# A root of one-tensor steps, and a new order of all operations and buffers, in a fused attention and two-layer kernel

## The chip, the cores and the metric

The kernel runs on one core of a Trainium2 chip. The metric is the device time of one execution in microseconds. Three runs of the kernel before took 750.36, 754.2 and 755.68 us; their median, 754.2 us, is what the change is measured against.

## The reference, cut to what matters

Windowed attention (4 batches, 8 heads, 576 positions, head size 64, window 128, a slope per head), then a layer with a softmax-weighted activation and a layer norm, then a second layer with a sigmoid gate. There are 2304 tokens of 512 numbers; the weights are float64 in memory.

```python
scores = scale * (q @ k.T) + slope * -|rel|, masked to 0 <= rel < 128
attn_out = softmax(scores) @ v                       # 2304 x 512
h = attn_out @ w_in                                  # 512 -> 1024
solu = h * softmax(h)
ln = (solu - mean(solu)) / np.sqrt(var(solu) + 1e-06) * g_ln
x2 = ln @ w_out                                      # 1024 -> 512
h2 = x2 @ w2_in                                      # 512 -> 2048
out = (h2 * (1 / (1 + np.exp(-h2)))) @ w2_out        # 2048 -> 512
```

## The kernel before, in words

**Numbers.** Every matmul operand is split into two fp16 parts, high and low, and a product takes three matmuls (high by high, high by low, low by high). The weights arrive as 64-bit words: `decode` (L404 to L411) makes float32 of them on DVE in three instructions per tile of 128x512, 48 tiles in all (8 of w_in, 8 of w_out, 16 of w2_in, 16 of w2_out). A weight's scale needs the norm over all of its tiles (squares on ACT, summed on PE at L449), so no tile of a matrix is split before the whole matrix is decoded. `split_weight` (L457) splits a tile in one of two ways, by a letter of `E_W`: V is one ACT instruction (L469) and one DVE instruction (L471); G is two ACT instructions (L475, L335) and one on POOL (L340).

**Stages.** The tokens are 18 blocks of 128. A block goes through attention (four pairs of heads: scores L599, bias and maximum L624, exp L629, high and low part of the result L335 with L339 or L340, a transposing DMA L656, product with v L676), is divided by its sums (xm, L689), split and transposed (x, L704, or on PE at L504), multiplied by w_in (L718), and normalised (`layer_norm`, L722 to L776). Two blocks make a chunk, nine chunks in all. A chunk is multiplied by w_out (`m1_out`, L808, into the tile y), then goes in eight groups through w2_in (`m2_in`, L845, gate at L854 to L858, into the tile g) and w2_out (`m2_out`, L872).

**The root in the layer norm.** The inverse root of the variance is a guess by bit operations (L747, L749) and three Newton steps, each of two `scalar_tensor_tensor` instructions on 128x1 tiles (L751, L753). Both have two tensors as inputs; L751 has a pointer to a scalar besides, L753 an immediate. L757 is of the form of L751.

**Order.** Every operation is recorded with a priority and with the engines that may do it, and a list planner on the host (`Sched.solve`, L178) gives out the order: at each moment the engine that can begin first takes the ready operation with the lowest priority number. The priority is `PITCH * i + RANK[kind]` for a block i, or a number of `WAT` for weight tiles (the first for load and decode, the third for the split). DMAs are issued by SP, in the same order. `ENG` chooses, per block, whether the subtraction for the low part of a (attention), x or l (normalised rows) goes to V (DVE), G (POOL) or B (the planner chooses); `ON_PE` chooses per block whether x or l is transposed on PE (P) or by DMA (D). The `N_...` constants are the numbers of buffers of a tile: a buffer is written again only when all readers of its last contents are done. For a group of `m2_in` that is a buffer of PSUM ("mm", 2), one of t (`N_T`), one of g (`N_G`); for a chunk one of lnT and one of y.

## Time and profile before

| | |
|---|---|
| median of three runs | 754.2 us |
| the profiled execution | 753.94 us, span 752.2 us, mean granted clock 0.972 |
| PE busy | 679.7 us (90%) |
| DVE busy | 467.9 us (62%) |
| ACT busy | 392.6 us (52%) |
| POOL busy | 68.4 us (9%) |
| chain that ended last | PE 73%, DVE 15%, DMA 5%, ACT 3% |

The span is what the profile covers, from the first instruction to the last; the execution's own time has 1.7 us more. Busy shares are means over the whole span; in slices of a fortieth, PE stands at 2 to 6 tenths in the first slices and at 9 from the ninth on (with an 8 in the tenth and in the last), and DVE the other way round, at 8 or 9 in most of the first third and at 1 to 3 at the end.

### The profile page before, as it was taken

The numbers are of one execution on the slowest core, as the hardware profiler recorded it, in microseconds if no ns is written. First come the engines' busy times: TensorE is split into PE (matmuls) and PEld (weight loads), VectorE is DVE, ScalarE is ACT, GpSimd is POOL, SyncE is SP. The second block draws the span as 40 slices with busy tenths as digits, with TensorE's granted clock in tenths as the row PEclk, the third lists the DMA queues.
The fourth block names the chain that finished last, engine by engine and source line by source line (L and its number), as shares of the span: only waits on it lengthen the run. The fifth ranks groups of instructions, "written<-read, shape, count | busy, mean of one in ns | idle before, by whom it ended". The sixth has DMA issues, their size and how long they took to land.

```text
span 752.2 us, 13817 instructions
## 1 busy us (share of the span) xinstructions
PE 679.7 (90%) x5366; PEld 453.7 (60%) x5366; DVE 467.9 (62%) x1259; ACT 392.6 (52%) x843; POOL 68.4 (9%) x63
## 2 busy tenths in 40 slices
PE   2445568898999999999999999999999999999998
PEld 1121235676764776567675775686666768767763
DVE  5998989989999867645466546646553272322221
ACT  6588558777677765444363535634661251322231
POOL 0053013312213000000020000000110000000000
PEclk9998668999999999999999999999999999999999
DMA  8997896579753646055342350464232300300000
GB/s 233 283 261 210 248 241 129 131 195 199 186 99 84 155 98 148 1 93 121 69 99 58 85 99 15 99 120 78 57 85 51 62 30 1 57 29 1 1 29 29
DMA packets 144034, 80.28 MB, mean 107 GB/s; under 512 B 125920, under 2 KB 126560, under 8 KB 143968
## 3 DMA queue, kind: packets, MB, share of 16 engines
q1 hardware_dynamic: 143968, 79.39, 44.9%
q8 instruction: 42, 0.69, 0.4%
q14 instruction: 24, 0.20, 0.1%
HBM read 44.24 MB, written 4.72 MB: 65 GB/s over the span
## 4 chain that ended last, share of the span: by engine, by line
PE 73%; DVE 15%; DMA 5%; ACT 3%; issue 2%; SPq 1%; POOL 0%; DVEq 0%; ACTq 0%; POOLq 0%
PE mm L872 23%; PE mm L845 22%; PE mm L808 11%; PE mm L718 9%; PE sa L599 4%; PE sa L676 3%; DMA stage<-in_moe_w_in_dram 2%; DVE bits L407 2%; DVE bits L409 2%; DVE W L411 2%; DVE e L624 2%; DMA aT<-a 1%; DMA stage<-in_moe_w_out_dram 1%; DVE W L471 1%; DVE e L739 1%
## 5 line engine op out<-in xcount | busy, mean ns | idle before, releaser
L845 PE MATMUL mm<-y,W 128*128 128x256 f16 x1728 | 208.4, 273 | 3.4 <-DVE t L855 2.0
L872 PE MATMUL mm<-W,g 128*128 128x512 f16 x864 | 206.8, 379 | 0.0
L845 PEld LDWEIGHTS <-W 128*128 128x128 f16 x1728 | 166.2, 98 | 41.4 <-issue 3.8
L872 PEld LDWEIGHTS <-g 128*128 128x128 f16 x864 | 81.8, 98 | 78.7 <-issue 0.6
L718 PE MATMUL mm<-W,xT 128*128 128x512 f16 x432 | 107.3, 395 | 1.6 <-ACT xT L506 1.3
L808 PE MATMUL mm<-lnT,W 128*128 128x256 f16 x864 | 106.9, 276 | 0.0
L808 PEld LDWEIGHTS <-W 128*128 128x128 f16 x864 | 84.2, 99 | 18.7 <-issue 0.3
L629 ACT ACTIVATE e<-e,mx 128x256 f32<-128x256 f32 (+1 forms) x144 | 70.0, 487 | 34.7 <-DVE mx L624 34.4
L599 PEld LDWEIGHTS sa<-k,q 64*128 64x128 f32 x544 | 41.6, 209 | 62.9 <-DVE mx L624 34.2
L857 ACT ACTIVATE g<-t 128x512 f16<-128x512 f32 x72 | 44.9, 625 | 66.2 <-PE mm L872 54.1
L858 DVE SCALAR_TENSOR_TENSOR g<-t,g 128x512 f16<-128x512 f32 x72 | 49.5, 688 | 47.4 <-ACT g L857 47.0
L855 DVE SCALAR_TENSOR_TENSOR t<-t,mm 128x512 f32<-128x512 f32 x72 | 48.8, 683 | 47.0 <-ACT t L854 47.0
L599 PE MATMUL sa<-k,q 64*128 64x128 f32 x544 | 57.1, 329 | 19.2 <-DVE mx L624 13.1
L718 PEld LDWEIGHTS <-xT 128*128 128x128 f16 x432 | 42.1, 101 | 51.8 <-issue 8.0
L854 ACT ACTIVATE t<-mm,cs 128x512 f32<-128x512 f32 x72 | 48.5, 679 | 46.5 <-PE mm L845 46.4
L624 DVE CUSTOM_DVE_ANT_0 e<-sa,table 128x256 f32<-128x256 f32 (+1 forms) x144 | 55.7, 404 | 23.6 <-PE sa L599 9.7
L335 ACT ACTIVATE a<-e 128x512 f16<-128x512 f32 (+1 forms) x72 | 43.1, 598 | 36.2 <-DMA aT<-a 35.9
L340 POOL TENSOR_TENSOR a<-e,a 128x512 f16<-128x512 f32 x24 | 29.0, 1210 | 290.9 <-ACT a L335 256.6
L449 PE MATMUL mm<-sq,ones 128*128 128x512 bf16 x32 | 17.0, 537 | 39.2 <-ACT sq L439 32.1
L339 DVE TENSOR_TENSOR a<-e,a 128x512 f16<-128x512 f32 (+1 forms) x48 | 31.5, 656 | 26.3 <-ACT a L335 26.3
L816 DVE SCALAR_TENSOR_TENSOR y<-mm,cs,y 128x512 f16<-128x512 f32 x18 | 13.4, 748 | 48.9 <-ACT y L813 48.9
L813 ACT ACTIVATE y<-mm,cs 128x512 f16<-128x512 f32 x18 | 12.3, 686 | 57.2 <-PE mm L808 49.1
(124 smaller groups left out, 698.0 us busy)
## 6 DMA issues: line engine op xcount, KB each, us to landing
stage<-in_moe_w_in_dram SPq DMA_DIRECT2D x24, 512.0 KB, 5.1
stage<-in_moe_w_out_dram SPq DMA_DIRECT2D x24, 512.0 KB, 4.2
vraw<-in_vt_dram SPq DMA_DIRECT2D x34, 256.0 KB, 3.4
k<-in_kn_dram SPq DMA_DIRECT2D x18, 256.0 KB, 3.1
q<-in_qn_dram SPq DMA_DIRECT2D x18, 256.0 KB, 3.5
out_dram<-t SPq DMA_DIRECT2D x18, 256.0 KB, 2.0
aT<-a SPq DMA_TRANSPOSE x72, 3.1
lnT<-ln SPq DMA_TRANSPOSE x34, 3.2
```

Source lines behind the costliest of these rows:

```text
L335: "A": ("A", ca(n), lambda: A.activation(dst(), src(), AF.Copy), False)}
L599: T.matmul(SA[:, j, sl * P:(sl + 1) * P], q[rows, p, :], k[rows, p, :], start=True, stop=sl not in blank)
L624: v(n + 75, lambda j=j: V.tensor_tensor_reduce(e[:, j, lo:lo + n], SA[:, j, lo:lo + n], table[:, 2 * p + j, o:o + n], -0.125, 3.0e38, ALU. ...
L629: act(n, lambda j=j: A.activation(e[:, j, lo:lo + n], e[:, j, lo:lo + n], AF.Exp, bias=mx[:, j:j + 1], scale=-1.0, accum_out=rs[:, 2 * p + ...
L718: T.matmul(pt[:, half * 512:(half + 1) * 512], x[:, hx, k, :], W16(2 * k + half, hw), start=(k == 0 and hx + hw == 0), stop=(k == KD - 1 a ...
L808: T.matmul(pt[:, ct % 2], W16(8 + k, hw)[:, ct * P:(ct + 1) * P], l[:, hx * KF1 + k, :], start=(k == 0 and hw + hx == 0), stop=(k == KF1 - ...
L845: T.matmul(pt[:, mm], W16(16 + 4 * k + m // 4, hw)[:, (m % 4) * P:(m % 4 + 1) * P], y[:, hx, k, :], start=(k == 0 and hw + hx == 0), stop= ...
L854: act(512, lambda: A.activation(t.tile, flat(pt.tile), AF.Tanh, scale=cs[:, 0:1]), [pt, (cs, 0)], [t], extra=1)
L855: v(512, lambda: V.scalar_tensor_tensor(out=t.tile, in0=t.tile, scalar=1.0, in1=flat(pt.tile), op0=ALU.add, op1=ALU.mult), [t, pt], [t])
L857: act(512, lambda: A.activation(flat(g[:, 0]), t.tile, AF.Copy, scale=2.0 ** -16), [t], [(g, 0)])
L858: v(512, lambda: V.scalar_tensor_tensor(out=flat(g[:, 1]), in0=t.tile, scalar=2.0 ** -16, in1=flat(g[:, 0]), op0=ALU.mult, op1=ALU.subtrac ...
L872: T.matmul(pt.tile, g[:, hg, mm, b * P:(b + 1) * P], W16(32 + m, hw), start=(m == 0 and hg + hw == 0), stop=(m == KF2 - 1 and hg == 1))
```

## The change

The root's steps become `tensor_scalar` instructions: one tensor and two scalars, of which both are pointers in the first step (var and y) and one in the second (y). The sign that the reversed subtraction gave moves into the constant in front of the steps. The instruction that makes `share` (L757) takes the same form. The planner's costs of five kinds of instruction are changed, and all numbers that set the order: pitch, ranks, the weights' priorities, the choices of engine, the numbers of buffers and `AHEAD`. The table of biases gets a rank of its own. Nothing else of the computation changes.

```diff
@@ -481,6 +481,7 @@
 
 
     def make_table():
+        s.at("table", 0)
         r = Buf(early, [P, 512, 2], U32, "stage", N_STAGE)
 
         def rl():
@@ -561,7 +562,7 @@
         sv = rows_of(i, v_scale, "sv")
         r = vraw.pop(i)
         act(512, lambda: A.activation(t[:, :, 0, :], r.tile, AF.Identity, scale=sv.tile), [r, sv], [(t, 0)], extra=1)
-        v(570, lambda: V.scalar_tensor_tensor(out=t[:, :, 1, :], in0=r.tile, scalar=sv.tile, in1=t[:, :, 0, :],
+        v(640, lambda: V.scalar_tensor_tensor(out=t[:, :, 1, :], in0=r.tile, scalar=sv.tile, in1=t[:, :, 0, :],
                                               op0=ALU.mult, op1=ALU.subtract), [r, sv, (t, 0)], [(t, 1)], port=True)
 
 
@@ -621,7 +622,7 @@
         else:
             lo, n, o = cur, P, P
         for j in range(2):
-            v(n + 75, lambda j=j: V.tensor_tensor_reduce(
+            v(n + 20, lambda j=j: V.tensor_tensor_reduce(
                 e[:, j, lo:lo + n], SA[:, j, lo:lo + n], table[:, 2 * p + j, o:o + n], -0.125, 3.0e38,
                 ALU.add, ALU.min, mx[:, j:j + 1]), [(SA, ("s", j)), (table, 2 * p + j)], [(e, j), (mx, j)])
         s.at("exp", i, p)
@@ -729,7 +730,7 @@
         if i % 2 == 0:
             share[i // 2] = Buf(const, [P, 2], F32, "share", 2)
         sh = share[i // 2]
-        v(1024, lambda: V.tensor_reduce(mx(), pt.tile, AX.X, ALU.max), [pt], [st])
+        v(1090, lambda: V.tensor_reduce(mx(), pt.tile, AX.X, ALU.max), [pt], [st])
         v(60, lambda: V.tensor_scalar(mx(), mx(), sg[:, 1:2], None, ALU.mult), [st, sg], [st])
         act(1024, lambda: A.activation(e.tile, pt.tile, AF.Exp, bias=mx(), scale=sg[:, 0:1], accum_out=sm()),
             [pt, st, sg], [e, st], extra=2.6)
@@ -746,16 +747,14 @@
           [st], [st])
         v(1, lambda: V.tensor_scalar(y().bitcast(U32), var().bitcast(U32), 1, 0x7FFFFFFF,
                                      ALU.logical_shift_right, ALU.bitwise_xor), [st], [st])
-        v(1, lambda: V.tensor_scalar(y(), y(), 0.7 * 2.0 ** -65.5, None, ALU.mult), [st], [st])
+
+        v(1, lambda: V.tensor_scalar(y(), y(), -0.7 * 2.0 ** -65.5, None, ALU.mult), [st], [st])
         for _ in range(3):
-            v(110, lambda: V.scalar_tensor_tensor(out=w(), in0=y(), scalar=var(), in1=y(), op0=ALU.mult,
-                                                  op1=ALU.mult), [st], [st])
-            v(80, lambda: V.scalar_tensor_tensor(out=y(), in0=w(), scalar=1.5, in1=y(), op0=ALU.subtract,
-                                                 op1=ALU.mult, reverse0=True), [st], [st])
-        v(1240, lambda: V.tensor_scalar(e.tile, e.tile, tot(), y(), ALU.add, ALU.mult), [e, st], [e], fast=True)
-
-        v(100, lambda: V.scalar_tensor_tensor(out=sh[:, i % 2:i % 2 + 1], in0=y(), scalar=sq(), in1=y(), op0=ALU.mult,
-                                              op1=ALU.mult), [st], [(sh, i % 2)])
+            v(80, lambda: V.tensor_scalar(w(), y(), var(), y(), ALU.mult, ALU.mult), [st], [st])
+            v(80, lambda: V.tensor_scalar(y(), w(), 1.5, y(), ALU.subtract, ALU.mult), [st], [st])
+        v(1380, lambda: V.tensor_scalar(e.tile, e.tile, tot(), y(), ALU.add, ALU.mult), [e, st], [e], fast=True)
+
+        v(80, lambda: V.tensor_scalar(sh[:, i % 2:i % 2 + 1], y(), sq(), y(), ALU.mult, ALU.mult), [st], [(sh, i % 2)])
         c = i // 2
         if i % 2 == 0:
             lnT[c] = Buf(const, [P, 2 * KF1, 2 * P], F16, "lnT", N_LNT)
@@ -893,7 +892,6 @@
     v_norm(0)
     s.prio = -50.0
     load(4, lambda: SP.dma_start(gcol.tile, g_ln.rearrange("(k p) -> p k", p=P)), [], [gcol])
-    s.prio = -10.0
     make_table()
     load_weight("win", w_in, 0, 8, FF1)
     v_sigma(0)
@@ -954,17 +952,17 @@
 
 
 
-PITCH = 11.32
-RANK = {"vnorm": 49.3, "vload": 484.2, "vsplit": 33.7, "load": -172.6, "qk": 64.5, "max": -18.1, "exp": 177.0,
-        "parts": -264.2, "aturn": 8.5, "av": -72.1, "evac": -293.9, "xturn": -54.8, "in": -50.0, "max1": -124.5,
-        "norm": -18.1, "lparts": -393.1, "out": -65.5, "share": -394.5, "y": -220.0, "in2": 114.9, "gate": 73.8,
-        "out2": 151.8, "store": -85.9}
-
-
-
-
-WAT = {0: (63.4, 0.0, 47.9, 0.0), 8: (-37.9, 0.0, -224.6, 0.0), 16: (-30.4, 0.0, 77.6, 0.0),
-       32: (79.9, 0.0, 11.7, 0.0)}
+PITCH = 4.63
+RANK = {"table": 21.4, "vnorm": 16.9, "vload": 471.3, "vsplit": 21.1, "load": -135.3, "qk": -14.9, "max": -83.8,
+        "exp": 345.6, "parts": -269.5, "aturn": -19.0, "av": 192.4, "evac": -366.3, "xturn": -204.5,
+        "in": -248.2, "max1": -1.8, "norm": -179.4, "lparts": -333.0, "out": -59.6, "share": -330.5, "y": -102.6,
+        "in2": 82.3, "gate": -185.4, "out2": 210.8, "store": -154.3}
+
+
+
+
+WAT = {0: (41.6, 0.0, 110.9, 0.0), 8: (-115.1, 0.0, -261.1, 0.0), 16: (18.8, 0.0, 119.0, 0.0),
+       32: (125.6, 0.0, 23.9, 0.0)}
 
 
 def WEIGHT(slot0, at, split=False):
@@ -975,11 +973,11 @@
 LAG = 2
 NSLOT = 48
 TB = 256
-E_W = "GGGGGVGVVVGVGVVGGGGGVVGVGVGVVVGGVVVVVGGGGVVGVVVV"
-
-ENG = {"a": "BGGGBGGBBBVVBBBBGB", "x": "BBVGGGBBBBVVVVVVBB", "l": "BBVGBGBBBGGBVBBBBV"}
-
-ON_PE = {"a": "DDDDDDDDDDDDDDDDDD", "x": "PDPPDPDDDDDDDDDDDD", "l": "DDPDDDDDDDDDDDDDDD"}
+E_W = "GGGGVGGGVGVVGGGGVVGGGVGGVGGVGGVGVVGGVVVGVGVVGGVV"
+
+ENG = {"a": "GGGGGGBVBBBBGVVBBG", "x": "VVVGGBBGGGGBVVBBBB", "l": "BVVVVBBBBBBBVVVBBG"}
+
+ON_PE = {"a": "DDDDDDDDDDDDDDDDDD", "x": "PDPDDDDDDDDDDDDDDD", "l": "DPDPDDDDDDDDDDDDDD"}
 N_STAGE = 3
 N_VS = 2
 N_VRAW = 1
@@ -987,15 +985,15 @@
 N_Q = 1
 N_E = 3
 N_A16 = 1
-N_AT = 5
-N_XT = 4
+N_AT = 3
+N_XT = 1
 N_E1 = 1
-N_L16 = 1
+N_L16 = 3
 N_LNT = 1
-N_Y = 1
-N_T = 4
-N_G = 5
-AHEAD = 2
+N_Y = 2
+N_T = 5
+N_G = 3
+AHEAD = 1
 SKEW = 0
 NQ = NB
 V_AT = [0, 1, 5, 9]
```

## Rows read from the trace of the kernel before

**Rows 1.** Stretches: us, busy (x count) PE, PEld, DVE, ACT, POOL; PEclk, DMA share, GB/s.
```profile
0.00:60.00 60.00, 26.03 (x118) 12.57 (x119) 48.94 (x129) 41.20 (x101) 13.16 (x21) 1.00 0.94 260
60.00:160.00 100.00, 69.50 (x562) 43.96 (x561) 90.32 (x232) 72.03 (x157) 25.17 (x21) 0.80 0.76 191
160.00:250.00 90.00, 86.33 (x722) 58.17 (x721) 85.40 (x244) 70.87 (x166) 21.21 (x16) 1.00 0.63 143
250.00:752.20 502.20, 497.79 (x3968) 339.03 (x3966) 243.20 (x657) 208.52 (x422) 8.89 (x6) 1.00 0.30 65
740.00:752.20 12.20, 8.40 (x39) 3.63 (x37) 0.00 (x0) 1.37 (x2) 0.00 (x0) 0.96 0.11 43
```

**Rows 2.** The layer norm's small instructions, line by line: ns min/median/max.
```profile
L751 DVE SCALAR_TENSOR_TENSOR lnst<-lnst x54: 197/216/1118, 88.6 to 618.0; 128x1 f32<-128x1 f32 x54
L753 DVE SCALAR_TENSOR_TENSOR lnst<-lnst x54: 147/159/1130, 89.9 to 618.3; 128x1 f32<-128x1 f32 x54
L733 DVE TENSOR_SCALAR lnst<-lnst,sig x18: 196/207/216, 70.3 to 610.6; 128x1 f32<-128x1 f32 x18
L747 DVE TENSOR_SCALAR lnst<-lnst x18: 145/153/154, 83.1 to 616.8; 128x1 uint32<-128x1 uint32 x18
L755 DVE TENSOR_SCALAR e<-e,lnst x18: 798/809/815, 93.7 to 619.0; 128x1024 f32<-128x1024 f32 x18
```

**Rows 3.** L751 alone by stretch: busy us and instructions.
```profile
60.00:160.00 100.00, 2.79 (x9) 0.80 0.76 191
160.00:250.00 90.00, 3.54 (x12) 1.00 0.63 143
```

**Rows 4.** L753 alone by stretch: busy us and instructions.
```profile
60.00:160.00 100.00, 2.75 (x9) 0.80 0.76 191
160.00:250.00 90.00, 4.95 (x11) 1.00 0.63 143
```

**Rows 5.** DVE in order of time, one root: start, duration.
```profile
224.65 0.21 DVE L751 SCALAR_TENSOR_TENSOR lnst<-lnst 128x1 f32<-128x1 f32 x1
224.90 1.01 DVE L753 SCALAR_TENSOR_TENSOR lnst<-lnst 128x1 f32<-128x1 f32 x1
225.94 1.08 DVE L751 SCALAR_TENSOR_TENSOR lnst<-lnst 128x1 f32<-128x1 f32 x1
```

**Rows 6.** POOL in order of time, the same stretch.
```profile
224.74 3.39 POOL L340 TENSOR_TENSOR W<-W 128x512 f16<-128x512 f32 x3 [0.37 <-ACT W L335]
```

**Rows 7.** The weight split on DVE, w2_out and w2_in: ns min/median/max.
```profile
L471 DVE SCALAR_TENSOR_TENSOR W<-W,sw2out x11: 728/744/2360, 217.8 to 243.1; 128x512 f16<-128x512 f32 x11
L471 DVE SCALAR_TENSOR_TENSOR W<-W,sw2in x7: 699/744/754, 127.9 to 148.7; 128x512 f16<-128x512 f32 x7
```

**Rows 8.** Groups by line and shape: low parts on DVE; busy us, mean ns.
```profile
L339 DVE TENSOR_TENSOR a<-e,a 128x512 f16<-128x512 f32 x40 | 28.2, 705 | 26.0 <-ACT a L335 25.9
L339 DVE TENSOR_TENSOR ln<-e,ln 128x1024 f16<-128x1024 f32 x13 | 16.2, 1244 | 11.0 <-ACT ln L772 10.9
L339 DVE TENSOR_TENSOR x<-xm,x 128x512 f16<-128x512 f32 x13 | 8.9, 686 | 0.0
L339 DVE TENSOR_TENSOR a<-e,a 128x256 f16<-128x256 f32 x8 | 3.3, 413 | 0.3 <-ACT a L335 0.3
L507 DVE TENSOR_TENSOR lnT<-mm,lnT 128x512 f16<-128x512 f32 x2 | 1.4, 682 | 0.0
```

**Rows 9.** The same on POOL.
```profile
L340 POOL TENSOR_TENSOR a<-e,a 128x512 f16<-128x512 f32 x24 | 29.0, 1210 | 290.9 <-ACT a L335 256.6 <-DVE W L411 34.2
L340 POOL TENSOR_TENSOR W<-W 128x512 f16<-128x512 f32 x23 | 28.1, 1232 | 32.6 <-ACT W L335 32.6
```

**Rows 10.** A weight tile's first decode instruction, by stretch: busy us and instructions.
```profile
60.00:160.00 100.00, 13.00 (x19) 0.80 0.76 191
160.00:250.00 90.00, 6.85 (x10) 1.00 0.63 143
```

**Rows 11.** First and last start of the w2_out matmul; matmuls of w2_in before it.
```profile
L872 PE MATMUL mm<-W,g x864: 376/379/390, 218.9 to 748.0; 128*128 128x512 f16 x173
0.00:218.90 218.90, 31.98 (x264) 24.89 (x264) 0.91 0.81 205
```

## The prediction

> **What bounds the kernel now.** I read the busy time by stretch first, because a share over the whole span mixes two regimes. From 250 us on, PE is busy 497.8 of 502.2 us, and 3.8 of the 4.4 us that are missing lie behind the last matmul; DVE is busy for less than half of it [rows 1]. No order of the same matmuls makes that stretch shorter, so the change has to act before 250 us. There PE is idle for 34.0 us up to 60, 30.5 us from 60 to 160 and 3.7 us from 160 to 250, in sum 68.2 us. The engine that is full there is DVE: 90.3 of 100 us in the second stretch and 85.4 of 90 in the third [rows 1]. Part of that is decoding: 19 tiles begin between 60 and 160, each three instructions of 0.685 us, 2.05 us a tile and 39 us in all [rows 10]. In the same stretch the granted clock is 0.80 on average. As the clock has two levels, a mean of 0.80 of full speed says that 40% of the stretch was at the lower one; of PE's 69.5 us some 13.9 us are the price of that (69.5 x 0.20). At stake are thus about 68 us of idleness and 14 us of low clock, and of these the first 60 us, with scarcely any weights decoded, are hard to touch.
>
> **The root.** Seven layer norms fall before 250 us. L751 takes 216 ns by its median and L753 159 ns [rows 2], but their sums are larger: from 60 to 160 the nine L751 take 2.79 us against 9 x 0.216 = 1.94, and the nine L753 2.75 against 1.43; from 160 to 250, 3.54 against 2.59 and 4.95 against 1.75 [rows 3, 4]. That is 2.2 us of excess in the first stretch and 4.1 in the second. The order of time shows what it is: steps of 1.01 and 1.08 us beside a run of POOL instructions on the weights [rows 5, 6]. The `tensor_scalar` instructions of the same layer norm, eighteen each, never go over 216, 154 or 815 ns [rows 2]. So I take the excess as a two-tensor instruction's wait for POOL, and as gone with the change. What the new form adds: a second step with one pointer and one immediate has a row of its own form, 207 ns (L733), 48 ns more than L753. The first step, with two pointers, has no row on such a tile. A pointer costs 54 ns (L733's 207 against L747's 153), so the bounds are 207 and 261 ns; I take 216, what L751 costs with its pointer and its second tensor, being the nearest, and the same for L757. Three steps then add 0.14 us to a layer norm, up to 0.33 by the upper bound. Before 160 us: -2.2 + 3 x 0.14 = -1.8 us of DVE; from 160 to 250: -4.1 + 0.6 = -3.5 us.
>
> The page "SBUF — State Buffer" of the Trainium skill (Who interferes with whom) speaks against a part of this. It says that `tensor_scalar`, too, can enter a mode that uses both ports, and is then blocked by GpSimd for a whole instruction. By that, the new steps would wait as the old ones do, and the root would cost 0.14 us more per layer norm in place of saving; the row of L755, the one wide `tensor_scalar` between two SBUF tiles, with 815 ns at most, shows no such wait here. This is a rival below.
>
> **Splits.** In the new string 20 tiles are V, where 25 were: 4 fewer of the first 32 tiles, which the trace splits before 160 us, and 1 fewer of w2_out. DVE saves 0.744 us each [rows 7], 3.0 us before 160 and 0.7 after. Each costs ACT one instruction more and POOL 1.23 us [rows 9]. ACT is at 72 of 100 us and POOL at 25 of 100 from 60 to 160 [rows 1], which covers both. If POOL falls behind, a tile is late for its first matmul.
>
> **Low parts.** POOL did 24 of attention's in the old order, just the six blocks marked G, so B has gone to DVE each time, and I count it so. For blocks 0 to 6: attention's move off DVE for block 0 (4 x 0.413 = 1.7 us), while blocks 4 and 6 change places; x moves off it for block 3 (0.7 us); of the normalised rows, block 5 returns to DVE (+1.24), block 3 comes from POOL to PE's way (+1.36, two subtractions of 0.682), and blocks 1 and 2 change places [rows 8]. The sum is +0.2 us: nothing.
>
> **More work on POOL.** Five weight tiles, four small tiles and one x more, two wide tiles fewer: eight instructions net. In the old order the waits seen, 6.3 us of the root and 1.6 us of one split (2360 against 744 ns, [rows 7]), fall on 37 POOL instructions between 60 and 250 us [rows 1], 0.21 us each. Bounds for the eight: nothing (the root was the victim and is gone) to 1.7 us. I take 1 us, 0.7 of it before 160.
>
> **From DVE to the end.** Before 160: -1.8 - 3.0 + 0.7 = -4.1 us of DVE, and DVE is 90% busy while PE is idle, so I take 4 us of the end. From 160 to 250: -3.5 - 0.7 + 0.3 = -3.9 us; PE lacks only 3.7 us there, and I take 1 us. Bounds: 0 to 8 us.
>
> **The new order.** Old, w2_in's tiles (-30) stood before attention's maxima (-18 and up by block) and the norm; new, they (18.8) stand behind the maxima of all blocks (-84 to -5) and behind the norm, and w2_out (125.6) stays last. With a second buffer of y, a chunk can pass w_out before its predecessor has gone through w2_in. So between 60 and 160 us PE gets blocks where it waited for w2_in's decoding. That is no free gain: the 39 us of decoding are put off into a stretch where DVE is full already. What remains is that denser work on PE keeps the clock up. Bounds: 0 and the 13.9 us of low clock; I take a third, 5 us. The cases where the order costs time are the second and the third rival.
>
> **Edits counted at nothing.** The table's load goes behind the first load of v on SP; both stand before w_in's, as before, and the chain starts with w_in's. One buffer of xT where there were four and three of aT where there were five: from 250 us on a block comes every 45 us or so (502 us for eleven blocks) and PE has m2's groups beside it. If that cover is gone, PE waits for a transpose. `AHEAD` at 1 and three g: the last group's gate is hidden by the matmuls of two groups before it. The second step's added nanoseconds after 250 us: DVE is idle for half of that time. One more normalised block on POOL is block 17, when PE has the previous chunk's groups.
>
> **Sum.** The profiled execution took 753.94 us, 0.26 us under the median, so it stands for it. 754 - 4 - 1 - 5 = **744 us**; own range 734 to 750.
>
> **Rivals.**
> 1. *The steps still wait* (the Trainium skill's rule, as a mechanism here: POOL holds an instruction of one tensor as it holds one of two). The two root terms turn from -1.8 and -3.5 into +0.4 and +0.6; the DVE term shrinks from 5 to about 2 us: 747 us. Against it stand the maxima of L733, L747 and L755 [rows 2]. Chance 0.08.
> 2. *The front is fixed by DVE's sum.* The DVE time freed lies where PE is fed, and moving decoding only moves the gap. For it: PE's 96% from 160 to 250, and DVE full in both stretches [rows 1]. 753 us, range 747 to 758. Chance 0.22.
> 3. *Slower: PE runs dry before w2_out is ready.* Before the first w2_out matmul at 218.9 us PE had done 264 matmuls of w2_in, 11 groups of 24 [rows 11]: as many as five g, four t and two PSUM buffers hold. The new order has room for 3 + 5 + 2 = 10, while w2_out stands last on DVE. If eight of its tiles are left to decode when the tenth group is done, DVE needs 16 us at least, of which the second buffer of y can cover some 4: 754 + 12 = 766 us. It decides from the point where PE's store of groups is used up more than 4 us before w2_out's last tile. For it: 10 tiles were still decoded after 160 us in the old order, which put less ahead of them [rows 10]. Against it: the second y gives PE other work. Chance 0.2.
>
> **How the numbers follow.** The forecast keeps a chance of 0.5. Range 732 to 762: below lies the order's upper bound, above half of the third rival. A measurement of this kernel tells 1% from no change, 7.5 us: faster is below 746.7, slower above 761.7. Faster: nine tenths of the forecast and a third of the first rival, 0.48. Slower: three quarters of the third and the far ends of the others, 0.2. Same: 0.32.
>
> **What would show it.** Right: no step of the root above 0.3 us, in the changed trace, beside POOL's weight instructions; DVE's sum before 250 us down by some 8 us; PE's idle time from 60 to 160 below 27 us with a granted clock over 0.80 there; the stretch with PE full starting earlier. Wrong: PE idle between 160 and 260 us with w2_out's decoding on DVE (third rival), or gaps in PE after 250 us before matmuls on xT or aT, which I counted at nothing.

## The result, and the profile after

The changed kernel took 761.12 us (758.6 to 762.4, 6 runs) where the kernel before took 752.5 us in the same comparison (750.36 to 755.68, 6 runs): a ratio of 1.0106, 95% interval 1.0076 to 1.0136, 8.6 us slower by the medians. I had forecast 744 us and gave "faster" the largest chance; 761.12 lies at the upper end of the range. The profiled execution took 758.6 us, the fastest of the six, with a span of 756.8 us and a mean granted clock of 0.968. Its span is 4.6 us longer than the one before, so the rows below account for 4.6 of the 8.6 us.

**By stretch.** This is the changed kernel's answer to [rows 1], with the same columns.

```profile
0.00:60.00 60.00, 21.26 (x101) 10.75 (x102) 43.99 (x116) 39.13 (x96) 15.07 (x24) 1.00 0.86 252
60.00:160.00 100.00, 70.82 (x530) 42.88 (x530) 91.64 (x234) 74.03 (x163) 35.84 (x30) 0.76 0.77 196
160.00:250.00 90.00, 86.16 (x744) 60.33 (x742) 76.85 (x217) 66.43 (x149) 15.60 (x13) 1.00 0.56 128
250.00:756.80 506.80, 500.55 (x3995) 338.48 (x3993) 257.56 (x677) 215.30 (x443) 17.62 (x14) 1.00 0.31 67
```

From 250 us on PE is full again. Of the 4.6 us by which the span grew, 2.8 us are PE work that was left at 250 us (500.55 against 497.79), and 1.8 us are more idle time behind that point (6.25 against 4.41). So most of this loss was made before 250 us. PE's idle time up to 60 us is 38.7 us (34.0 before), then 29.2 (30.5), then 3.8 (3.7). The mean clock from 60 to 160 us is 0.76 where it was 0.80: of the 70.82 us of busy time more ran at the lower level, so that more busy time there is not more work.

DVE's sum up to 250 us fell by 12.2 us, from 224.7 to 212.5, more than the 8 us that I had named as the sign of success. Yet the whole of DVE rose from 467.9 to 470.0 us, since the last stretch took 14.4 us more. In sum DVE was not relieved; work that it did before 250 us now comes later, and PE had less to do early on.

**The root.** The answer to [rows 2]: ns minimum, median and maximum of each line. The first step is L753 now and the second L754; L755 and L757 keep their numbers.

```profile
L753 DVE TENSOR_SCALAR lnst<-lnst x54: 259/272/274, 79.2 to 672.8; 128x1 f32<-128x1 f32 x54
L754 DVE TENSOR_SCALAR lnst<-lnst x54: 196/214/215, 80.0 to 673.1; 128x1 f32<-128x1 f32 x54
L755 DVE TENSOR_SCALAR e<-e,lnst x18: 802/812/1095, 84.9 to 673.4; 128x1024 f32<-128x1024 f32 x18
L757 DVE TENSOR_SCALAR share<-lnst x18: 261/267/271, 85.6 to 674.1; 128x1 f32<-128x1 f32 x18
```

None of the 126 small instructions (54, 54 and 18) takes over 274 ns, where single ones had taken 1118 and 1130 ns. The waits for POOL went out of the root, as forecast. One place shows both kinds of `tensor_scalar` beside POOL; DVE in order of time (start, duration) and then POOL:

```profile
228.59 0.27 DVE L753 TENSOR_SCALAR lnst<-lnst 128x1 f32<-128x1 f32 x1
228.89 0.21 DVE L754 TENSOR_SCALAR lnst<-lnst 128x1 f32<-128x1 f32 x1
229.14 1.09 DVE L755 TENSOR_SCALAR e<-e,lnst 128x1024 f32<-128x1024 f32 x1
```

```profile
228.37 1.31 POOL L340 TENSOR_TENSOR W<-W 128x512 f16<-128x512 f32 x1 [1.11 <-ACT W L335]
```

The two small steps run while POOL is in its instruction (228.37 to 229.68 us) and take what they always take; the wide L755 begins within it and takes 1.09 us instead of 0.81. The Trainium skill's page "SBUF — State Buffer" (Who interferes with whom) says that `tensor_scalar` can enter a mode that GpSimd blocks. The trace agrees for the wide one, by 0.28 us here, though POOL's instruction ran on for 0.54 us after L755's start, and the one-element steps were not held up. It was the only L755 of 18 beside a POOL instruction. In the kernel before none of the 18 was, so the maximum of 815 ns that I had set against the first rival could not show a wait. With the new root in the old order (e2 below) one began beside POOL at 226.46 us and took 1595 ns:

```profile
L755 DVE TENSOR_SCALAR e<-e,lnst x18: 799/810/1595, 95.0 to 620.0; 128x1024 f32<-128x1024 f32 x18
```

The weight splits on DVE wait as well, at other places than before. For w2_in the maximum was 754 ns and for w2_out 2360 [rows 7]; now it is the other way round:

```profile
L471 DVE SCALAR_TENSOR_TENSOR W<-W,sw2out x10: 733/744/751, 212.6 to 240.1; 128x512 f16<-128x512 f32 x10
L471 DVE SCALAR_TENSOR_TENSOR W<-W,sw2in x6: 736/1039/1587, 123.0 to 150.4; 128x512 f16<-128x512 f32 x6
```

Summed over all splits before 250 us, the time above 744 ns each is 2.6 us in 20 splits, where it was 2.2 us in 25: about as much as before.

**The blocks.** The most telling rows are the first matmuls of w_in for a block, since everything behind attention hangs on them. PE in order of time (start, duration), blocks 0, 1 and 3, of the kernel before:

```profile
55.88 1.03 PE L718 MATMUL mm<-W,xT 128*128 128x512 f16 x2 [1.25 <-ACT xT L506]
...
90.55 4.05 PE L718 MATMUL mm<-W,xT 128*128 128x512 f16 x9
...
145.10 5.68 PE L718 MATMUL mm<-W,xT 128*128 128x512 f16 x21
```

and of the changed one:

```profile
60.42 7.17 PE L719 MATMUL mm<-W,xT 128*128 128x512 f16 x24
...
100.17 4.45 PE L719 MATMUL mm<-W,xT 128*128 128x512 f16 x10 [1.29 <-DMA xT<-x]
...
153.22 5.34 PE L719 MATMUL mm<-W,xT 128*128 128x512 f16 x24
```

Block 0 is 4.5 us late, block 1 9.6 us, block 3 8.1 us. Between block 0 and block 1 PE has little to do, and it shows in the granted clock. Stretches of 20 us, with the columns of [rows 1], of the kernel before and then of the changed one:

```profile
80.00:100.00 20.00, 14.08 (x121) 7.92 (x119) 17.11 (x43) 9.98 (x22) 2.32 (x2) 0.77 1.01 259
```

```profile
80.00:100.00 20.00, 8.26 (x75) 5.05 (x74) 17.89 (x46) 9.41 (x19) 2.31 (x2) 0.50 1.03 235
```

A mean of 0.50 is the lower level for the whole stretch; in it PE did 75 matmuls where it had done 121.

**Why block 1 is late.** SP's transposing DMAs for aT (the weights of the softmax, transposed) show it. Four belong to a block, one for each pair of heads. SP in order of time, the third and fourth of block 0 and the fourth of block 1, before:

```profile
26.67 1.19 SPq L656 DMA_TRANSPOSE aT<-a  x1
31.38 1.19 SPq L656 DMA_TRANSPOSE aT<-a  x1
...
60.35 1.23 SPq L656 DMA_TRANSPOSE aT<-a  x1
```

The same of the changed kernel:

```profile
26.50 1.19 SPq L657 DMA_TRANSPOSE aT<-a  x1
44.74 1.19 SPq L657 DMA_TRANSPOSE aT<-a  x1
...
84.37 1.64 SPq L657 DMA_TRANSPOSE aT<-a  x1
```

With three buffers of aT the fourth transpose must wait until a product with v has read one, and that product needs v, whose scale is known only after a norm over the whole batch of v. PE's products with v in the changed kernel, in order of time:

```profile
40.71 0.21 PE L677 MATMUL sa<-vs,aT 128*128 128x64 f16 x1
44.24 1.06 PE L677 MATMUL sa<-vs,aT 128*128 128x64 f16 x17 [3.31 <-DVE vs L565]
```

So the fourth transpose of block 0 moves from 31.4 to 44.7 us, and the fourth of block 1 from 60.4 to 84.4. The kernel before issues the load of block 1's own v at 74.31 us and the changed one at 74.74; what is late in the changed one is the transpose. I had counted N_AT from 5 to 3 at nothing and looked only behind 250 us for its cover. SP's waits over the whole run (what stood in its queue, what it waited for, us in total, times, longest):

```profile
SPq L574 <- PE sa L600: 89.7, 14, 14.7
SPq L657 <- PE sa L677: 64.0, 13, 13.7
```

The second row, a transpose that waits for a free buffer of aT, has no counterpart in the kernel before. The first, the load of k, waited 14.0 us there; in the changed kernel with five aT (f1 below) it waits 11.9.

**What did not happen.** The first matmul of w2_out starts at 217.0 us (218.9 before, [rows 11]), and PE lacks 3.8 us from 160 to 250 us: no dry spell before w2_out, the third rival. Behind 250 us, one gap that I had listed as a sign against me did show, small:

```profile
PE mm L719 <- DMA xT<-x: 1.6, 2, 1.3
```

### The profile page after: what moved, and what is told of

Read it like the earlier page. It is cut to its first block, busy times and chain, and to the rows that moved or that the text cites. A ratio compares the mean times of both kernels' runs of the same rounds, so it can differ in the third digit from the quotient of the medians.

```text
span 756.8 us, 13814 instructions
## 1 busy us (share of the span) xinstructions
PE 678.8 (90%) x5366; PEld 452.4 (60%) x5366; DVE 470.0 (62%) x1241; ACT 394.9 (52%) x850; POOL 84.1 (11%) x81
## 4 chain that ended last, share of the span: by engine, by line
PE 73%; DVE 11%; DMA 11%; ACT 3%; issue 2%; SPq 0%; POOL 0%; DVEq 0%; ACTq 0%
PE mm L871 22%; PE mm L844 20%; PE mm L719 12%; PE mm L807 11%; PE sa L600 4%; DMA xT<-x 3%; DMA aT<-a 3%; PE sa L677 2%; DMA stage<-in_moe_w_in_dram 2%; DMA stage<-in_moe_w_out_dram 2%; DVE W L411 2%; DVE bits L407 2%; DVE bits L409 1%; DVE e L625 1%; DMA vraw<-in_vt_dram 1%
## 5 line engine op out<-in xcount | busy, mean ns | idle before, releaser
L844 PE MATMUL mm<-y,W 128*128 128x256 f16 x1728 | 214.1, 273 | 1.9 <-DVE y L815 1.9
L871 PE MATMUL mm<-W,g 128*128 128x512 f16 x864 | 210.3, 379 | 0.0
L844 PEld LDWEIGHTS <-W 128*128 128x128 f16 x1728 | 165.1, 98 | 44.7 <-issue 2.6
L719 PE MATMUL mm<-W,xT 128*128 128x512 f16 x432 | 102.0, 393 | 5.3 <-DMA xT<-x 5.3
L857 DVE SCALAR_TENSOR_TENSOR g<-t,g 128x512 f16<-128x512 f32 x72 | 52.8, 735 | 78.2 <-ACT g L856 77.9
L807 PE MATMUL mm<-lnT,W 128*128 128x256 f16 x864 | 100.3, 273 | 0.0
L600 PE MATMUL sa<-k,q 64*128 64x128 f32 x544 | 56.5, 327 | 21.3 <-DVE mx L625 15.0
L340 POOL TENSOR_TENSOR a<-e,a 128x512 f16<-128x512 f32 (+1 forms) x34 | 37.5, 1102 | 329.3 <-ACT a L335 329.3
L677 PEld LDWEIGHTS <-aT 128*128 128x128 f16 x816 | 33.3, 102 | 26.8 <-issue 9.8
L339 DVE TENSOR_TENSOR a<-e,a 128x512 f16<-128x512 f32 (+1 forms) x38 | 26.0, 685 | 28.2 <-ACT a L335 28.2
L677 PE MATMUL sa<-vs,aT 128*128 128x64 f16 x816 | 35.9, 199 | 6.3 <-DVE vs L565 3.3
```

Source lines behind the costliest of these rows:

```text
L600: T.matmul(SA[:, j, sl * P:(sl + 1) * P], q[rows, p, :], k[rows, p, :], start=True, stop=sl not in blank)
L677: T.matmul(heads()[:, h // 4, h % 4, :], t[:, (2 * ha + j) * nh + c, :], vb[sl][:, h, hv, :], start=(n == 0), stop=(n == 3 * nh - 1))
L719: T.matmul(pt[:, half * 512:(half + 1) * 512], x[:, hx, k, :], W16(2 * k + half, hw), start=(k == 0 and hx + hw == 0), stop=(k == KD - 1 a ...
L807: T.matmul(pt[:, ct % 2], W16(8 + k, hw)[:, ct * P:(ct + 1) * P], l[:, hx * KF1 + k, :], start=(k == 0 and hw + hx == 0), stop=(k == KF1 - ...
L844: T.matmul(pt[:, mm], W16(16 + 4 * k + m // 4, hw)[:, (m % 4) * P:(m % 4 + 1) * P], y[:, hx, k, :], start=(k == 0 and hw + hx == 0), stop= ...
L857: v(512, lambda: V.scalar_tensor_tensor(out=flat(g[:, 1]), in0=t.tile, scalar=2.0 ** -16, in1=flat(g[:, 0]), op0=ALU.mult, op1=ALU.subtrac ...
```

## The experiments

Times stand as ratios to the kernel before on the same chip, with 95% intervals. Beside them I use one figure of my own: **work**, the matmuls begun by a moment, each counted at about its spacing at full clock (0.109 us for 256 columns, 0.216 for 512, and 0.04 to 0.16 for the smaller shapes). The counts come from stretches of 10 us, and a matmul across their border counts twice. The two large spacings are those of stretches where PE is full, as here in the changed kernel (24 matmuls of w2_in in 514.17 - 511.54 = 2.63 us; 24 of w_in in 520.30 - 515.01 = 5.29 us):

```profile
511.54 2.79 PE L844 MATMUL mm<-y,W 128*128 128x256 f16 x24
514.17 0.81 PE L871 MATMUL mm<-W,g 128*128 128x512 f16 x3
515.01 5.35 PE L719 MATMUL mm<-W,xT 128*128 128x512 f16 x24
520.30 0.71 PE L600 MATMUL sa<-k,q 64*128 64x128 f32 x8
```

So it is an estimate, good to a few per cent and for differences. Its use is this: span plus work by 260 us is 923 to 928 us in every kernel but one below (h1, 930), so the state at 260 us decides the end, and the column shows where a kernel lost. The diffs below are cut to the lines that matter.

| kernel | ratio | work by 120 / 160 / 260 us | span |
|---|---|---|---|
| before | 1 | 40.3 / 72.5 / 171.6 | 752.2 |
| changed | 1.0106 | 33.0 / 68.4 / 168.3 | 756.8 |
| new order alone (k1) | 1.0184 | 33.2 / 61.5 / 158.4 | 765.8 |
| aT 3 in the old numbers (g1) | 1.0238 | 32.3 / 62.9 / 155.6 | 769.0 |
| all new buffers in the old numbers (g4) | 1.0321 | 32.0 / 64.2 / 151.1 | 772.9 |
| changed, v's norm later (h1) | 1.0191 | 42.0 / 67.7 / 163.9 | 766.3 |

### Root, splits and order, each with the others held

Here the order is held exactly: every instruction stands where the planner had put it, and only the form of the root, or the engine of a split, is exchanged. An exchanged split thus stands at a place that was planned for the other engine. First the new order with the root of before (e1); the sign of the constant and `share` go back too:

```diff
-            v(80, lambda: V.tensor_scalar(w(), y(), var(), y(), ALU.mult, ALU.mult), [st], [st])
-            v(80, lambda: V.tensor_scalar(y(), w(), 1.5, y(), ALU.subtract, ALU.mult), [st], [st])
+            v(80, lambda: V.scalar_tensor_tensor(out=w(), in0=y(), scalar=var(), in1=y(), op0=ALU.mult, op1=ALU.mult), [st], [st])
+            v(80, lambda: V.scalar_tensor_tensor(out=y(), in0=w(), scalar=1.5, in1=y(), op0=ALU.subtract, op1=ALU.mult, reverse0=True), [st], [st])
```

> The changed kernel with the root's three steps and the share instruction put back to two-tensor instructions, every instruction in the same place as in the changed kernel. Theory A (the wait for POOL does not go away with the root's new form, it moves to the next two-tensor instruction, and DVE is not what ends the front there): within 2 us of the changed kernel, a ratio to before of 1.008 to 1.013. Theory B (the root's form saves the 5 us that I predicted, and the order loses more than it shows): 4 to 6 us slower than the changed kernel, ratio 1.016 to 1.019. Theory C (two-pointer steps cost more than they save, 0.27 us against 0.22): 1 to 3 us faster, ratio 1.006 to 1.009.

Measured: 1.0167 (1.0151 to 1.0182), theory B by its number. The root's waits are back:

```profile
L753 DVE SCALAR_TENSOR_TENSOR lnst<-lnst x54: 205/219/1115, 79.9 to 678.3; 128x1 f32<-128x1 f32 x54
L754 DVE SCALAR_TENSOR_TENSOR lnst<-lnst x54: 146/159/845, 80.7 to 678.6; 128x1 f32<-128x1 f32 x54
```

Then the old order with the new root (e2; the reverse of that diff, in the kernel before):

> The kernel before with the root's new form alone, every instruction in its old place. Theory A: 751 to 754 us, ratio 0.998 to 1.002. Theory B: the excess of 6.3 us in the old root's steps before 250 us goes, 4 us of it before the stretch where PE is full: ratio 0.993 to 0.996. Theory C: ratio 1.001 to 1.004.

Measured: 0.9985 (0.9973 to 0.9996), 1.1 us, theory A, and the only kernel of the study below the one before. In this order DVE did not get the 5.3 us that I had reckoned before 250 us: its sum there fell by 2.8 us, from 224.65 to 221.82. The waits of 6.3 us went, but the new steps cost more than I had put on them, L755's wait is new, and the waits of the splits grew by 0.7 us. Its two steps:

```profile
L751 DVE TENSOR_SCALAR lnst<-lnst x54: 258/270/274, 89.7 to 618.9; 128x1 f32<-128x1 f32 x54
L753 DVE TENSOR_SCALAR lnst<-lnst x54: 200/210/215, 91.1 to 619.2; 128x1 f32<-128x1 f32 x54
```

The new order with the split letters of before (e4; five more tiles on DVE; at the place of the old letter the other letter's instructions are issued):

```diff
+DONE = "GGGGGVGVVVGVGVVGGGGGVVGVGVGVVVGGVVVVVGGGGVVGVVVV"
+                is_v = DONE[b] == "V"
+                    act(512, hi_only if is_v else both, [(W, a), src], [(W, b)], extra=1)
+                    v(560, lo_v if is_v else lo_g, [(W, a), (W, b), src], [(W, b)], port=True)
```

> The changed kernel, same order, but each weight tile is split by the engine that the kernel before uses for it (25 on DVE, 23 on POOL, in place of 20 and 28); each instruction stands where its planned counterpart stands. Theory A (POOL's queue is in order, and attention's low parts wait behind weight tiles there, so that the splits moved to POOL lengthen the front): 2 to 5 us faster than the changed kernel, ratio 1.004 to 1.008. My prediction's step (DVE ends the front, and each split on POOL frees 0.74 us of it): 3 us slower, ratio 1.013 to 1.016.

Measured: 1.0180 (1.0165 to 1.0195), slower than either expectation had it. The new order with both put back (k1; the two diffs together):

> The new order with its buffers alone: the root and the share in their old form of two tensors, the splits on the engines of the kernel before. Theory A (the order alone costs what the root and the splits give back; the two gains add): before plus about 18 us (8.6 + 4.5 + 5.6), near 771 us, ratio 1.024, with 260 us reached with about 153 us of matmul work done (168.3 in the changed kernel, 171.6 before). Theory B (the two gains are one and the same relief of VectorE, so they don't add): near 767 us, ratio 1.018 to 1.020, as each of the two kernels with one of the edits undone. Theory C (my prediction's term): the order itself gains, ratio below 1.

Measured: 1.0184 (1.0165 to 1.0202), 13.9 us of 752.9: the price of order and buffers by themselves. By its number that is theory B, but not by its reason, as the table below shows. The old order with the new letters, with the new root (k2) and without it (k3; the second diff, `DONE` now the new string):

> The order and the buffers of the kernel before, with the new root and share and with the five splits of weights on POOL. Theory A (root and splits each save VectorE's time where VectorE holds TensorE up, in any order): 752.5 - 1 for the root, and up to 5 for the splits, 746 to 751 us, ratio 0.992 to 0.998, POOL's splits hidden. Theory B (in the old order VectorE is not what TensorE waits for, so that the splits give nothing): 0.998 to 1.000. Theory C (POOL's longer splits make its later instructions and what waits for them late in the old order): above 1.000.

> The order, buffers and root of the kernel before, with the five splits of weights on POOL alone. Theory A: ratio 0.993 to 0.999, the kernel with root and splits lying about 1 us below it. Theory C (POOL late): above 1.000.

Measured: 1.0048 (1.0031 to 1.0064) and 1.0035 (1.0020 to 1.0050): theory C; the splits cost time in the old order. DVE was nevertheless relieved there. Its stretch up to 250 us, in the columns of [rows 1], of the kernel before and of k2:

```profile
0.00:250.00 250.00, 181.87 (x1400) 114.70 (x1401) 224.65 (x604) 184.09 (x422) 59.54 (x57) 0.92 0.75 190
```

```profile
0.00:250.00 250.00, 178.54 (x1387) 113.05 (x1388) 215.88 (x588) 186.38 (x421) 63.92 (x62) 0.92 0.75 188
```

In the same order DVE's sum is 8.8 us lower, more than my sign of success asked for, and the time is 3.6 us longer. All ratios together:

| | root old, splits old | root new | splits new | both new |
|---|---|---|---|---|
| old order | 1 | 0.9985 | 1.0035 | 1.0048 |
| new order | 1.0184 | 1.0180 | 1.0167 | 1.0106 |

Neither edit has a price of its own. In the new order each alone takes 1.3 us or less off, which the intervals do not tell from nothing, and both together 0.8%, 5.9 us. The rows show where. Block 3's matmuls of w_in, which start at 153.22 us in the changed kernel, in e1, e4 and k1, one fence each:

```profile
161.60 5.34 PE L719 MATMUL mm<-W,xT 128*128 128x512 f16 x24
```

```profile
161.48 5.34 PE L735 MATMUL mm<-W,xT 128*128 128x512 f16 x24
```

```profile
161.30 5.34 PE L735 MATMUL mm<-W,xT 128*128 128x512 f16 x24
```

All three are 8 us later than the changed kernel, and equally late, though block 2's, at 125.6, 126.7 and 127.3 us, are only 1.7 to 3.3 us behind its 123.9. The stretch ahead of block 3, first of the changed kernel, then of e1 and of k1:

```profile
140.00:160.00 20.00, 17.37 (x160) 12.06 (x159) 19.00 (x44) 16.90 (x42) 11.15 (x9) 1.00 0.78 172
```

```profile
140.00:160.00 20.00, 15.81 (x137) 12.03 (x135) 18.87 (x40) 16.20 (x40) 11.54 (x9) 0.77 0.64 162
```

```profile
140.00:160.00 20.00, 15.79 (x147) 12.35 (x146) 18.86 (x38) 17.46 (x43) 10.52 (x8) 0.83 0.53 137
```

With both edits PE is idle for 2.6 of the 20 us and the clock stays up; with one or both missing it is idle for 4.2 (e1, k1), and the granted clock is 0.77 or 0.83. In finer stretches the idleness comes first: from 148 to 153 us PE is busy for 4.71 us in the changed kernel, 2.39 in e1, 1.24 in e4 and 1.21 in k1, and from 153 to 158 us the granted clock is 1.00 in the changed kernel and 0.50 in the other three. That a small delay here is made larger by the clock's fall fits these rows; no kernel changed the clock alone, so I call it likely, not shown.

Of the loss in the old order the rows show the place only. In k3, PE's first matmul of w_in comes 2.5 us late (55.88 before), and still waits for ACT:

```profile
58.41 7.09 PE L734 MATMUL mm<-W,xT 128*128 128x512 f16 x21 [1.98 <-ACT xT L522]
```

A tile that moves to POOL costs ACT one instruction more, and ACT has this evacuation in its queue: in k3 it runs with hardly a gap from 49.4 us to the evacuation at 57.78 (55.26 before). But ACT is 1.0 us late by 42 us already, before it scales the first tile of w_in, and POOL's low parts of attention come about 1 us later too (45.16 us for 44.12, 52.56 for 51.47); no run separates these.

### The buffers

More buffers in the exact new order, so that only the waits for them could go (e3):

```diff
+MORE = {"xT": 2, "aT": 4}
-                    x.tile = x.pool.open.tile(list(x.shape), x.dtype, tag=x.tag, bufs=x.n, name=x.tag)
+                    x.tile = x.pool.open.tile(list(x.shape), x.dtype, tag=x.tag, bufs=MORE.get(x.tag, x.n), name=x.tag)
```

> The changed kernel, same order, with two buffers of xT (planned for one) and four of aT (planned for three). If the single xT holds up the transposes that come late: PE's gaps after 250 us (2.6 us, against 0.6 before) close, 2 us faster than the changed kernel, ratio 1.007 to 1.009. If the transposes are late because the DMA queue gives them out late, in its own order: no change, ratio 1.009 to 1.013.

Measured: 1.0104 (1.0087 to 1.0122), the same as the changed kernel. Its fourth transpose still comes at 45.03 us: the load of v that stands ahead of it in SP's queue goes out at 44.65. The planner has written the wait into the order, and a buffer that comes free earlier is not used earlier. So the next ones were planned anew. Three buffers of aT in the kernel before (g1):

```diff
-N_AT = 5
+N_AT = 3
```

> The kernel before with three buffers of aT in place of five, planned anew with that one number. Theory F: the fourth pair of block 0 waits for v's norm and the fourth of block 1 for block 1's v, as in the changed kernel: PE's matmuls of the first 60 us shrink by some 2 us of work, block 1 reaches w_in late, and the time goes up by 3 to 8 us, ratio 1.004 to 1.011. If the ranks are at fault and not the buffers: 0.997 to 1.003.

Measured: 1.0238 (1.0208 to 1.0268), 18 us, more than twice what theory F had at most. SP's transposes in it, as shown above for the two kernels:

```profile
26.99 1.20 SPq L656 DMA_TRANSPOSE aT<-a  x1
44.15 1.19 SPq L656 DMA_TRANSPOSE aT<-a  x1
...
84.92 1.30 SPq L656 DMA_TRANSPOSE aT<-a  x1
```

These are the changed kernel's times, in a kernel that shares its aT alone, and its stretch has the same clock and nearly the same matmuls:

```profile
80.00:100.00 20.00, 9.18 (x71) 5.10 (x71) 17.05 (x39) 10.21 (x21) 1.16 (x1) 0.50 0.80 209
```

All new buffers in the old numbers (aT 3, xT 1, ln 3, y 2, t 5, g 3, `AHEAD` 1), g4:

> The kernel before planned with all the numbers of buffers of the changed one (aT 3, xT 1, ln 3, y 2, t 5, g 3, AHEAD 1), all else as before. Theory A (the buffers, which I counted at nothing, cost the order its time): ratio near the one of the new order alone, 1.015 to 1.025, as with aT 3 alone (1.024). Theory B (the second y and the third buffer of ln make up for the others): 1.000 to 1.010.

Measured: 1.0321 (1.0302 to 1.0341), above both expectations. One buffer of xT in the exact old order (m2):

```diff
+FEWER = {"xT": 1}
```

> The kernel before in its exact order, only with one buffer of xT where it had four. My prediction counted this edit at nothing. Theory A (counted rightly): ratio 0.999 to 1.001. Theory B (a block's transpose then waits until the block before it has been through w_in, 7.8 us at the lower clock in the stretch before 160 us): one such wait before 160 us, 4 to 8 us, ratio 1.005 to 1.010.

Measured: 1.0005 (0.9992 to 1.0018). xT was rightly counted at nothing; aT was not. No run has three aT in the exact old order. The other way round, the changed kernel planned with five aT (f1), and with all buffers of before (f4, the reverse of g4's list); f1's diff:

```diff
-N_AT = 3
+N_AT = 5
```

> The changed kernel with five buffers of aT in place of three, planned anew with that one number. Theory D (three buffers of aT: before v's norm is known no product with v can run, so only three of attention's pairs can be transposed ahead, later ones stand in SP's queue in front of weight loads, and the first block's way to w_in is late): 6 to 12 us faster than the changed kernel, ratio 0.995 to 1.003. Theory E (the ranks and weight priorities as a whole put the work in a worse order, no one buffer does): ratio 1.005 to 1.02.

> The changed kernel with all buffer numbers and AHEAD of the kernel before (five aT, four xT, one l16, one y, four t, five g), planned anew. Theory D, buffers at fault: ratio 0.985 to 1.000. Theory E, ranks at fault: the ranks were chosen for other buffers, ratio 1.005 to 1.03. My prediction counted on the second buffer of y for part of its 5 us: without it 1.012 to 1.02.

Measured: 1.0136 (1.0109 to 1.0164) and 1.0079 (1.0050 to 1.0109), both in theory E's range; neither interval stands clear of the changed kernel's. In f1 the cause that I had found is gone and the time is not better. The fourth transpose is back, and yet block 1 comes to w_in no earlier; SP first, then PE:

```profile
32.69 1.19 SPq L657 DMA_TRANSPOSE aT<-a  x1
```

```profile
101.16 7.06 PE L719 MATMUL mm<-W,xT 128*128 128x512 f16 x24 [0.57 <-DMA xT<-x]
```

So the new numbers hold block 1 up a second time. In f1 block 1's own v is late: its load is issued at 81.97 us (74.31 before, 74.74 in the changed kernel). It goes behind the five loads for the second norm of v, through the one buffer that v has. That order alone is not the fault, since the kernel before has the same; there the fifth of them is issued at 69.46 us, and in f1 at 78.82. What holds them up in f1, no run tests.

### The numbers of the order

The changed kernel planned with the ranks and pitch of before, with the weight priorities of before, and with the engines of before (f2, f3, f5):

```diff
-PITCH = 4.63
+PITCH = 11.32
```

> The changed kernel with the pitch and the ranks of the kernel before (and the bias table loaded where it was), planned anew; weights' priorities, letters and buffers are the changed ones. Theory E, ranks at fault: ratio 0.985 to 1.000. Theory D, buffers at fault: 1.008 to 1.03.

```diff
-WAT = {0: (41.6, 0.0, 110.9, 0.0), 8: (-115.1, 0.0, -261.1, 0.0), 16: (18.8, 0.0, 119.0, 0.0),
-       32: (125.6, 0.0, 23.9, 0.0)}
+WAT = {0: (63.4, 0.0, 47.9, 0.0), 8: (-37.9, 0.0, -224.6, 0.0), 16: (-30.4, 0.0, 77.6, 0.0),
+       32: (79.9, 0.0, 11.7, 0.0)}
```

> The changed kernel with the weight tiles' priorities of the kernel before, planned anew: w2_in is decoded ahead of attention's maxima again. If putting w2_in behind attention is what lowers the clock between 80 and 118 us: ratio 0.99 to 1.003, and the long low stretch is broken up. If it does nothing: 1.006 to 1.015. If it helps, as I predicted: 1.015 to 1.03.

```diff
-ENG = {"a": "GGGGGGBVBBBBGVVBBG", "x": "VVVGGBBGGGGBVVBBBB", "l": "BVVVVBBBBBBBVVVBBG"}
+ENG = {"a": "BGGGBGGBBBVVBBBBGB", "x": "BBVGGGBBBBVVVVVVBB", "l": "BBVGBGBBBGGBVBBBBV"}
```

> The changed kernel planned with the engines of the kernel before for the low parts and for the transposes (ENG, ON_PE), all else as changed. Theory A (attention's low part of block 0 and 1 on POOL, behind the splits of weights, is what makes the new front late): below the changed kernel, ratio 0.998 to 1.006. Theory B (no single number is the cause; the string fits only the order it was chosen with): at or above the changed kernel, ratio 1.010 to 1.020.

Measured: 1.0213 (1.0177 to 1.0249), 1.0172 (1.0139 to 1.0206) and 1.0166 (1.0148 to 1.0184). Each of the three is slower than the changed kernel: no single one of them carries the loss, and putting POOL's low parts for block 0 back does not win time (theory A of the last). f3 lies in the range that I had given to the case that w2_in's decoding behind attention helps, as the prediction said.

Last, v's second norm put off (`V_AT`, the block at which each of four norms of v is planned), which should clear block 1's way: in the changed kernel, in the changed kernel with five aT, and in the kernel before with the new root (h1, h2, h3).

```diff
-V_AT = [0, 1, 5, 9]
+V_AT = [0, 3, 5, 9]
```

> The changed kernel with the norm of v's second batch at block 3 in place of block 1, three aT as it stands, planned anew. Theory F: block 1's v comes earlier, and with it a free aT; 2 to 6 us faster than the changed kernel, ratio 1.002 to 1.008. Theory E: 1.008 to 1.02.

> The changed kernel with five aT and with the norm of the second batch of v computed at block 3 in place of block 1 (it is first needed at block 4), planned anew. Theory F (block 1 reaches w_in at 100 us in place of 91 because four transposed pairs and block 1's v must both be there first: with three aT the fourth pair is late, and with five aT alone block 1's v is late, since it is loaded behind the five loads of the second norm through one buffer): block 1 at w_in by 93 us, and 5 to 9 us faster than the changed kernel, ratio 0.999 to 1.004. Theory E (any other plan of these ranks loses elsewhere what it wins here): 1.005 to 1.015.

> The kernel before with the root's new form and the norm of v's second batch at block 3 in place of block 1, planned anew. If these five loads, squares and the wait behind them hold up block 1 in the old order too: block 1 at w_in before 88 us, ratio 0.985 to 0.995. If the old order hides them: 0.997 to 1.003. If they only move into a fuller stretch: 1.003 to 1.01.

Measured: 1.0191 (1.0162 to 1.0221), 1.0247 (1.0221 to 1.0273), 1.0137 (1.0111 to 1.0163): h1 is in theory E's range, the other two are slower than any expectation. In h1 the front is cured: block 1 comes to w_in 14 us earlier, and work by 120 us is 42.0 us, more than before.

```profile
85.85 7.22 PE L719 MATMUL mm<-W,xT 128*128 128x512 f16 x24 [2.27 <-DMA xT<-x]
```

But by 160 us it has 67.7 and by 260 us 163.9 (72.5 and 171.6 before), and it ends later than the changed kernel. What the front gained was given back before 260 us, while DVE was busy for 89.4 of 100 us (60 to 160) and 76.6 of 90 (160 to 250); and behind 250 us PE is idle for 10.3 us, 6.3 in the changed kernel.

## Why the prediction was wrong

**The reading of the bound: right.** Behind 250 us PE is idle for 4 to 8 us in every kernel but h1 (10.3), and the end follows from what was done by then.

**The root: right in mechanism, its size depends on the order.** No step waits for POOL; the first rival is refuted. Of the three rows that I had set against it, L755's had no instance beside POOL, and L733 and L747 had one each. The two-pointer form costs 272 ns, above my upper bound of 261; I had taken 216 (the second step came at 214 for 207). I had put 1.8 + 3.5 us of DVE time on it. In the old order, where those waits were read, it gave 1.1 us; in the new order next to nothing without the splits (1.0184 to 1.0180), and 0.6% with them (1.0167 to 1.0106). For the 1 us that I took for more work on POOL the rows have 0.8 us where I looked: before 250 us the splits waited 0.5 us longer in sum, and L755 0.28 us.

**The splits: wrong for the old order.** I took 3.7 us of DVE as gained and POOL and ACT as cover. In the old order they cost 2.6 us (k3), and 4.7 us beside the new root (1.0048 against 0.9985); in the new order, beside the new root, they gain 5.6 us (1.0180 to 1.0106). Five is a net count, too: 15 tiles left DVE and 10 came to it. The cover was read from busy shares over 100 us, and a share does not say whether ACT is free at the moment when block 0 needs its evacuation.

**From DVE to the end: the step that turns DVE's time into PE's does not hold.** In the old order, held exactly, both edits took 8.8 us off DVE's sum before 250 us and the time rose by 3.6 us (k2). In the changed kernel DVE did 12.2 us less and PE 3.6 us less too, not more. Such a sum also falls when work merely comes later, and an engine at 90% beside an idle PE need not be what PE waits for. That root and splits together gave 5.9 us in the new order, near the 5 us that I had summed for DVE, is luck: DVE's sum before 250 us is 213.3 us in k1 and 212.5 in the changed kernel, and either edit alone gave next to nothing.

**The new order, -5 us: the step that failed.** With its buffers it cost 13.9 us (k1), where I had taken 5 us off. I had expected denser work on PE from 60 to 160 us, with a clock above 0.80 and idle time below 27 us; the rows have 0.76 and 29.2 us. Denser work needs blocks that have come out of attention, and blocks 1 and 3 are 8 to 10 us late.

**Edits counted at nothing: aT was not nothing.** Its cover behind 250 us is real (PE waits there for an aT once, 0.4 us); I did not look for one before 45 us, where the reader of aT waits for v's norm. Alone it costs 18 us in the old numbers, where the planner puts the whole order around it. xT was nothing, as counted, in the old order (m2), and a second xT beside a fourth aT gave nothing in the new one (e3).

**The rivals.** The third gave nearly the right time (766 us against 761.12) by a mechanism that did not occur. That the range held 761.12 at all is luck: its upper end came from half of that rival. The second comes nearest to the lesson of h1, that a gap cured in front comes back later, but it priced the change at 753 us and had no term for a front that gets worse.

**Open.** The loss is the new order's, and three buffers of aT explain its first 60 us: PE is busy there for 21.3 us in the changed kernel and 21.2 in g1, for 26.0 in the kernel before and 25.3 in f1. Of what holds block 1 up after that, f1 shows its v coming late, and h1 and h2 that an earlier block 1 does not make the kernel end earlier. No kernel with one group of numbers put back beats the changed one by more than the 2 us of f4, which the intervals do not tell from nothing. The five costs that the planner reckons with, and the split letters as the planner sees them, were put back in no run that was planned anew. The numbers were chosen together, and these runs do not split the 13.9 us among them. The best kernel of the study is the old order with the new root, 0.9985 of the time before.

## What to carry to other kernels

A buffer count is free only if the reader that empties it can already run: look for the moment when that reader first becomes able to, not only at the steady stretch. Price a new form of instruction within the order that it will stand in, and hold the order exactly while exchanging the form; here the new root gave 1.1 us in one order, and in another nothing or 0.6%, by what stood beside it. When a string of planner numbers changes together, one number put back tells little, since both sides were chosen as wholes.

## What the runs showed of the hardware

A `tensor_scalar` on a 128x1 tile took 272 ns with two pointers and 214 with one in the changed kernel, 153 with immediates alone in the kernel before (L747, on uint32) [rows 2]; the two-tensor form took 216 and 159 ns by its median, so that the new form is slower by itself by some 55 ns a step and gains only by its maximum, 274 against 1130 ns. Its maximum holds even where a step runs within a POOL instruction, while a wide `tensor_scalar` over 128x1024 elements rose from 812 ns by its median to 1095 ns there, and in e2 from 810 to 1595 ns. And a late block shows in TensorE's clock: from 80 to 100 us the granted clock was 0.50, the lower level throughout, in the changed kernel and in g1, which both have three buffers of aT, and 0.77 in the kernel before; PE did 75, 71 and 121 matmuls there. Five buffers do not undo it by themselves: f1 has 0.59 in that stretch, with 74 matmuls.
